# Attention products half a slot later, and output rows that alternate between two accumulators

## The chip, the core and the metric

The kernel runs on one core of one Trainium2 chip. The metric is device time in microseconds (us). Engines are named as in the profile: PE is TensorE (PEld its weight loads), DVE is VectorE, ACT is ScalarE, POOL is GpSimd, SP issues the DMAs. "L354" is line 354 of the kernel before.

## What is computed

A transformer block: attention with 32 query heads over cached keys and values, then a gated MLP, both behind a modulated layer norm.

```python
x = A_x                                         # (1, 2048, 576)
mod = (silu(c) @ w_mod).reshape(1, 6, 1, -1)    # shifts sa, sb, scales ca, cb, gates ga, gb
h = layernorm(x) * (1 + ca) + sa
q = (h @ wq) per head                           # 32 heads of 128
k, v = the last 512 rows of the caches          # 16 heads, each for two query heads
o = softmax(q k^T / sqrt(128)) v
x = x + ga * (o @ wo)
h = layernorm(x) * (1 + cb) + sb
x = x + gb * ((silu(h @ w1) * (h @ w3)) @ w2)   # 576 -> 4608 -> 576
```

All matrices are float32. The kernel splits each operand into a high and a low half of float16 and adds three products (high by high, high by low, low by high).

## The kernel before

The order of the instructions on every engine is the order in which the code issues them; each engine works its own list strictly in turn and waits where an operand or a buffer isn't ready.

Attention goes through 128 **slots**. A slot `i` is one query head on one block of 512 rows (`slots[i] = (u, j, b)`: group `u` of one key head, `j` which of its two query heads, `b` the block). Slots come in pairs, `j = 0` and `j = 1` on the same block. A slot has four **quarters** `t` (128 rows each). The main loop issues, per quarter:

- `scores(i, t)` (L401): three matmuls of `qT` with the keys into a PSUM bank; then DVE takes the maximum of each row (L405) and scales it (L406).
- `normalize(i - 2)` in the second quarter, DVE: for `j = 0` the low half of the values' product (L486), whose high half `take_first` makes on ACT (L479, first quarter); for `j = 1` the product times the inverse sums (L489), which `split_on` splits in the fourth quarter (L505, L506).
- `query_low(i + 1)` in the fourth quarter (L391, DVE): the low half of the next slot's `qT`.
- `weights(i, t)` (L418, ACT): the exponent, from the PSUM bank of the scores into `p`. `half_high` (L443, ACT) and `half_low` (L448, POOL) split `p` into `hp`, of which there are four buffers.
- `query(i + 1, t)` in the first three quarters (L343, L347): 14 matmuls of the next slot's projection into one bank (`pq`); with the last of them the high half of `qT` on ACT (L385).
- `attend_out` (L354, `back`): six matmuls that multiply one 128-row piece of an earlier pair with the output weights, into the accumulator `E` (`pe`, two PSUM banks). A row of the pair takes two pieces, one for each head; after the second, DVE adds the row to `acc` (L514). Second pieces fall in the second and fourth quarter.
- tasks at `(i, t)`: everything else that a table puts at that place: loads, peaks and scalings of weights, the making of the MLP's weights. Sums over partitions (L247, L1051, L1084) are matmuls into columns of `E` that the output rows don't use.
- `turn_away` (L455, SP): the DMA transposes of `hp` into `ptw`, two quarters after the scores. `ptw` has two buffers, one for a slot.

At the end of slot `i` comes `values(i - 1)` (L468): twelve matmuls of the values with `ptw` into a bank `po`. The PSUM's eight banks: two for `pq` and `po` (tag A), two for the scores of odd quarters (tag S), two for those of even quarters (`t_bank`, `pt`), two for `E`. `t_bank` also serves the transposes of the layer norm's rows in some slots.

The MLP's first products join in slot 127 (`stream`); after attention it has the rest of the time, and its down products alternate between `E` and two banks that replace `t_bank`'s.

Of the kernel before, what the change touches and what calls it, by code (L numbers as in the profile page):

```python
# [9 lines left out]
F32 = mybir.dt.float32  # L10
# [4 lines left out]
ALU = mybir.AluOpType  # L15
AX = mybir.AxisListType
PSUM = bass.MemoryType.PSUM
DRAM = bass.MemoryType.DRAM

P = 128  # L20
# [3 lines left out]
S = 2048  # L24
SB = 512
NSB = S // SB
ST = SB // P
# [5 lines left out]
HALF = D // 2  # L33
# [14 lines left out]
def tile_block(  # L48
# [19 lines left out]
    psum = ctx.enter_context(tc.tile_pool(name="psum", bufs=2, space=PSUM))  # L68
# [6 lines left out]
    def bank(tag, name):  # L75
        return psum.tile([P, 512], F32, tag=tag, name=name)


    E = psum.tile([P, 2, 512], F32, tag="E", name="pe", bufs=1)
    turning = ExitStack()  # L80
    tpool = turning.enter_context(tc.tile_pool(name="tpool", bufs=2, space=PSUM))

    def t_bank():
        return tpool.tile([P, 512], F32, tag="T", name="pt")

    def half_split(a):
        return a.rearrange("p (a n) -> p a n", a=2)
# [258 lines left out]
            else:  # L346
                nc.tensor.matmul(ps, w[:, k, DC, :], hT[:, 2 * DC, :], start=False, stop=k == 1)  # L347

    def back(o, w, t, first, last):

        rows = slice(t * P, (t + 1) * P)
        for n, (x, y) in enumerate(((0, 0), (0, 1), (1, 0))):
            for h in range(2):
                nc.tensor.matmul(  # L354
                    E[:, h, :HALF],
                    o[:, x, rows],
                    w[:, y, h * HALF : (h + 1) * HALF],
                    start=first and n == 0,
                    stop=last and n == 2,
                )  # L360
# [9 lines left out]
    slots = [(u, j, b) for u, (_, blocks, _) in enumerate(uses) for b in blocks for j in range(2)]  # L370
    begins = [next(i for i, slot in enumerate(slots) if slot[0] == u) for u in range(len(uses))]
    n = len(slots)
    state = [dict() for _ in range(n)]
    hT, wqs, keys, vals, wos = {}, {}, {}, {}, {}
# [14 lines left out]
    def query_low(i):  # L389
        q, ps = state[i]["qT"], state[i].pop("q")  # L390
        nc.vector.scalar_tensor_tensor(q[:, 1], ps, Q_DOWN, q[:, 0], op0=ALU.mult, op1=ALU.subtract)  # L391

    def scores(i, t):
        u, j, b = slots[i]
        g = uses[u][0]
        st = state[i]
        k, q = keys[u], st["qT"]
        rows = slice(t * P, (t + 1) * P)
        pss = bank("S", "pss") if t % 2 else t_bank()
        for n, (x, y) in enumerate(((0, 0), (0, 1), (1, 0))):  # L400
            nc.tensor.matmul(pss, q[:, x, rows], k[:, y, :], start=n == 0, stop=n == 2)  # L401
        m = (i * ST + t) % 3
        nm = nms[:, 2 * m : 2 * m + 2]
        factor = factors[:, g, j : j + 1]
        nc.vector.tensor_reduce(nm[:, 0:1], pss, axis=AX.X, op=ALU.max, negate=True)  # L405
        nc.vector.tensor_scalar(nm[:, 1:2], nm[:, 0:1], factor, P_LOG, op0=ALU.mult, op1=ALU.add)  # L406
        st["max", t] = pss, nm

    def weights(i, t):

        u, j, b = slots[i]
        factor = factors[:, uses[u][0], j : j + 1]
        st = state[i]
        pss, nm = st.pop(("max", t))
        if t == 0:
            st["l"] = odd.tile([P, 6 * ST], F32, tag="l", name="l", bufs=4) if j == 0 else state[i - 1]["l"]
        p = pool.tile([P, SB], F32, tag="p", name="p", bufs=PB)
        nc.scalar.activation(p, pss, AF.Exp, bias=nm[:, 1:2], scale=factor, accum_out=st["l"][:, j * ST + t : j * ST + t + 1])  # L418
        st["p", t] = p
# [20 lines left out]
    def half_high(i, t):  # L440

        hp = state[i]["hp", t] = pool.tile([P, 2, SB], F16, tag="hf", name="hp", bufs=HF)
        nc.scalar.copy(hp[:, 0, :], state[i]["p", t])  # L443

    def half_low(i, t):

        hp = state[i]["hp", t]
        nc.gpsimd.tensor_sub(hp[:, 1, :], state[i].pop(("p", t)), hp[:, 0, :])  # L448

    def turn_away(i, t):  # L450

        if t == 0:
            state[i]["pt"] = pool.tile([P, 2, KC, SB], F16, tag="pt", name="ptw")
        pt = state[i]["pt"]
        nc.sync.dma_start_transpose(  # L455
            out=pt.rearrange("p x c n -> p (x c) n")[:, :, t * P : (t + 1) * P],
            in_=state[i].pop(("hp", t)).rearrange("p x k -> p (x k)"),
        )

    def values(i):  # L460
        u, j, b = slots[i]
        st = state[i]
        v = vals[u]
        pt = st["pt"]
        po = bank("A", "po")
        for c in range(KC):
            for n, (x, y) in enumerate(((0, 0), (1, 0), (0, 1))):
                nc.tensor.matmul(  # L468
                    po, v[:, x, c, :], pt[:, y, c, :], start=c == 0 and n == 0, stop=c == KC - 1 and n == 2
                )  # L470
        st["po"] = po

    def new_o(i):
        return pool.tile([P, 2, SB], F16, tag=("ah", "al")[i % 2], name="o", bufs=3)

    def take_first(i):
        st = state[i]
        o = st["o"] = new_o(i)
        nc.scalar.activation(o[:, 0, :], st["po"], AF.Copy, scale=O_DOWN)  # L479

    def normalize(i):
        st = state[i]
        po = st.pop("po")
        if slots[i][1] == 0:
            o = st["o"]
            nc.vector.scalar_tensor_tensor(o[:, 1, :], po, O_DOWN, o[:, 0, :], op0=ALU.mult, op1=ALU.subtract)  # L486
            return
        on = st["on"] = pool.tile([P, SB], F32, tag="raw", name="on", bufs=RB)
        nc.vector.tensor_mul(  # L489
            on.rearrange("d (t p) -> d t p", t=ST),  # L490
            po.rearrange("d (t p) -> d t p", t=ST),
            st["r"].rearrange("d p t -> d t p"),
        )

    def split_on(i):
# [9 lines left out]
        nc.scalar.copy(o[:, 0, :], on)  # L505
        nc.gpsimd.tensor_sub(o[:, 1, :], on, o[:, 0, :])  # L506

    def attend_out(pair, t, j, total):
        u, _, b = slots[2 * pair]
        back(state[2 * pair + j]["o"], wos[u][:, j], t, j == 0, j == 1)  # L510
        if j == 1:
            run(*total)
            a = half_split(acc[b][:, t, :])
            nc.vector.scalar_tensor_tensor(  # L514
                a, E[:, :, :HALF], state[2 * pair]["l"][:, 5 * ST + t : 5 * ST + t + 1], a, op0=ALU.mult, op1=ALU.add
            )


# [457 lines left out]
    def run(i, t):  # L976
        for task, args in tasks.pop((i, t), ()):
            task(*args)
# [54 lines left out]
    lane = [0, ()]  # L1033
# [141 lines left out]
    for u, (g, blocks, whole) in enumerate(uses):  # L1175
# [8 lines left out]
        if u:  # L1184
            A = dict(load=-22, keys=-17, wq=-13, total=-9, scale=-9, put=-8, turn=-5, vals=-1)
            if u == 1:
                A.update(load=-16, keys=-13, wq=-13)
            A = {k: R + v for k, v in A.items()}
# [66 lines left out]
    for late in range(turns):  # L1255
        number = ITEMS + 4 * late
        loader, maker, w, _ = items[number]
        total = 2 * len(ORDER) * (late + 1) + ORDER.index("p3")
# [99 lines left out]
    for c in range(3):  # L1358
        i = 117 + 3 * c
# [112 lines left out]
    for i in range(n + 2):  # L1472
        run(i, -1)
        for t in range(ST):
            if t > 1 and i < n:
                turn_away(i, t - 2)
            if t < 2 and 1 <= i <= n:
                turn_away(i - 1, t + 2)
            if i < n:
                scores(i, t)  # L1480
            if 2 <= i <= n and t == 1:
                normalize(i - 2)
            if t == 3 and i + 1 < n:
                query_low(i + 1)
            if i < n:
                weights(i, t)
            if i < n:
                half_high(i, t)
                half_low(i, t)
            if 2 <= i <= n + 1 and t == 0 and slots[i - 2][1] == 0:  # L1490
                take_first(i - 2)
            if 1 <= i <= n and t < 2:
                sums(i - 1, t)
            if 2 <= i <= n and t == 3:
                split_on(i - 2)
            if i + 1 < n and t < ST - 1:
                query(i + 1, t)
            if i >= m0:
                for _ in range(3 if (i, t) == (n + 1, 0) else 1):
                    next(stream)  # L1500
            for piece in outs.get((i, t), ()):
                attend_out(*piece, (i, ("total", t)))
            run(i, ("total", t))
            run(i, ("taken", t))
            run(i, t)
            if 1 <= i <= n and t == 2:
                sums(i - 1, t)
            run(i, t)
        if 1 <= i <= n:
            values(i - 1)  # L1510
        if i == n:
            normalize(n - 1)
            split_on(n - 1)
    turning.close()
    after = ctx.enter_context(tc.tile_pool(name="after", bufs=1, space=PSUM))
    lane[1] = (E, after.tile([P, 2, 512], F32, tag="T2", name="pf"))
    for _ in stream:
        pass
    for i in (1, 0):
# [58 lines left out]
```

## Time and profile before

| | us |
|---|---|
| median of 3 runs | 2823.19 (2821.3 to 2827.48) |
| the profiled execution | 2823.43 |
| its span | 2821.6 |
| PE busy | 2678.1 (95%) |
| DVE busy | 1971.4 (70%) |
| ACT busy | 1637.1 (58%) |
| POOL busy | 1935.5 (69%) |

The span runs from the first to the last instruction. A busy time is the sum over an engine's instructions, without those that only wait or issue a DMA. In a row of a group, the count and the mean of one instruction stand behind the shapes, then the busy time, then the engine's idle time just ahead of these instructions with what ended it. A matmul's row shows 0.38 us for 512 columns, but the next one starts 0.22 us after it: they overlap, so the time that a row of matmuls takes is best read from start to start.

### The profile page before, as it was taken

The numbers are of one execution on the slowest core, as the hardware profiler recorded it, in microseconds if no ns is written. First come the engines' busy times: TensorE is split into PE (matmuls) and PEld (weight loads), VectorE is DVE, ScalarE is ACT, GpSimd is POOL, SyncE is SP. The second block draws the span as 40 slices with busy tenths as digits, with TensorE's granted clock in tenths as the row PEclk, the third lists the DMA queues.
The fourth block names the chain that finished last, engine by engine and source line by source line (L and its number), as shares of the span: only waits on it lengthen the run. The fifth ranks groups of instructions, "written<-read, shape, count | busy, mean of one in ns | idle before, by whom it ended". The sixth has DMA issues, their size and how long they took to land. (4 is left out here: it accounts for less than half of the span.)

```text
span 2821.6 us, 44006 instructions
## 1 busy us (share of the span) xinstructions
PE 2678.1 (95%) x15024; PEld 1480.2 (52%) x15024; DVE 1971.4 (70%) x3492; ACT 1637.1 (58%) x3022; POOL 1935.5 (69%) x1793
## 2 busy tenths in 40 slices
PE   6899999999999999999999899999999999999998
PEld 3455555555455554545554455555555555555555
DVE  6776777777778777777775548777776565656666
ACT  4687777778687877868676634544443333333332
POOL 4577788989799887877768726688874355334435
PEclk9999999999999999999999999999999999999999
DMA  5778888878798898989989954555644443333332
GB/s 168 178 169 186 202 197 183 194 173 207 157 195 196 191 207 179 226 175 225 212 195 215 200 162 159 191 185 190 213 136 125 148 127 122 109 104 109 104 111 76
DMA packets 711153, 479.86 MB, mean 170 GB/s; under 512 B 568080, under 2 KB 597904, under 8 KB 710160
## 3 DMA queue, kind: packets, MB, share of 16 engines
q1 hardware_dynamic: 710320, 477.05, 67.4%
q8 instruction: 118, 1.93, 0.3%
q14 instruction: 107, 0.88, 0.1%
q10 hardware_dynamic: 608, 0.00, 0.0%
HBM read 246.83 MB, written 95.86 MB: 121 GB/s over the span
## 5 line engine op out<-in xcount | busy, mean ns | idle before, releaser
L448 POOL TENSOR_TENSOR hp<-p,hp 128x512 f16<-128x512 f32 x512 | 595.0, 1166 | 292.0 <-ACT hp L443 159.0
L771 PEld LDWEIGHTS <-wset 128*128 128x128 f16 x3528 | 344.9, 98 | 336.8 <-issue 2.7
L354 PE MATMUL pe<-o 128*128 128x288 f16 x3072 | 464.2, 288 | 30.4 <-DVE acc L514 23.6
L771 PE MATMUL py<-hset,wset 128*128 128x512 f16 x2016 | 482.7, 380 | 1.8 <-ACT u L951 1.8
L468 PE MATMUL po<-ptw,v 128*128 128x512 f16 x1536 | 369.1, 392 | 61.0 <-DMA ptw<-hp 45.7
L354 PEld LDWEIGHTS <-o 128*128 128x128 f16 x3072 | 301.4, 98 | 210.1 <-issue 42.3
L418 ACT ACTIVATE p<-pt,table,factors 128x512 f32<-128x512 f32 x256 | 198.3, 775 | 324.0 <-DVE table L406 286.4
L771 PE MATMUL px<-hset,wset 128*128 128x512 f16 x1512 | 361.6, 379 | 0.0
L443 ACT CAST hp<-p 128x512 f16<-128x512 f32 x512 | 316.4, 618 | 35.7 <-DMA ptw<-hp 18.8
L92 POOL TENSOR_TENSOR akv<-u,akv 128x512 f16<-128x512 f32 x141 | 164.8, 1177 | 175.0 <-ACT akv L91 167.1
L405 DVE TENSOR_REDUCE table<-pss 128x1 f32<-128x512 f32 x256 | 176.1, 688 | 154.6 <-PE pss L401 154.4
L343 PE MATMUL pq<-hT,wq 128*128 128x512 f16 x1092 | 281.4, 380 | 0.0
L468 PEld LDWEIGHTS <-v 128*128 128x128 f16 x1536 | 151.7, 102 | 237.2 <-issue 63.7
L405 DVE TENSOR_REDUCE table<-pt 128x1 f32<-128x512 f32 x256 | 174.4, 681 | 90.5 <-PE pt L401 90.1
L418 ACT ACTIVATE p<-pss,table,factors 128x512 f32<-128x512 f32 x256 | 197.9, 773 | 35.9 <-DVE table L406 33.3
L856 PEld LDWEIGHTS <-akv 128*128 128x128 f16 x1728 | 169.2, 98 | 93.8 <-issue 4.5
L514 DVE SCALAR_TENSOR_TENSOR acc<-pe,l,acc 128x576 f32<-128x576 f32 x256 | 207.5, 811 | 15.5 <-PE pe L354 12.9
L401 PE MATMUL pt<-k,qT 128*128 128x512 f16 x768 | 210.9, 382 | 6.9 <-ACT qT L385 3.2
L401 PEld LDWEIGHTS <-qT 128*128 128x128 f16 x1536 | 151.0, 100 | 126.5 <-DVE qT L391 8.1
L401 PE MATMUL pss<-k,qT 128*128 128x512 f16 x768 | 212.2, 386 | 0.0
L343 PEld LDWEIGHTS <-wq 128*128 128x128 f16 x1104 | 108.4, 98 | 139.5 <-issue 9.8
L850 DVE SCALAR_TENSOR_TENSOR acc<-pf,table,acc 128x576 f32<-128x576 f32 x140 | 113.5, 811 | 80.6 <-PE pf L856 80.6
(232 smaller groups left out, 4738.5 us busy)
## 6 DMA issues: line engine op xcount, KB each, us to landing
wset<-wd SPq DMA_DIRECT2D x213, 320.0 KB, 3.2
oset<-od SPq DMA_DIRECT2D x106, 288.0 KB, 3.2
wraw<-in_w SPq DMA_DIRECT2D x36, 768.0 KB, 5.3
wd<-wmade SPq DMA_DIRECT2D x75, 320.0 KB, 3.3
r<-row SPq DMA_DIRECT2D x64, 256.0 KB, 4.0
wset<-wd SPq DMA_DIRECT2D x71, 160.0 KB, 2.2
w2raw<-in_w SPq DMA_DIRECT2D x19, 576.0 KB, 5.4
wd<-ring SPq DMA_DIRECT2D x33, 320.0 KB, 2.8
```

Source lines behind the costliest of these rows:

```text
L92: eng.tensor_sub(halves[:, 1], src, halves[:, 0])
L343: nc.tensor.matmul(ps, w[:, k // 2, m, :], hT[:, DC + m if k == 1 else m, :], start=s == 0, stop=False)
L354: nc.tensor.matmul(E[:, h, :HALF], o[:, x, rows], w[:, y, h * HALF : (h + 1) * HALF], start=first and n == 0, stop=last and n == 2,)
L401: nc.tensor.matmul(pss, q[:, x, rows], k[:, y, :], start=n == 0, stop=n == 2)
L405: nc.vector.tensor_reduce(nm[:, 0:1], pss, axis=AX.X, op=ALU.max, negate=True)
L418: nc.scalar.activation(p, pss, AF.Exp, bias=nm[:, 1:2], scale=factor, accum_out=st["l"][:, j * ST + t : j * ST + t + 1])
L443: nc.scalar.copy(hp[:, 0, :], state[i]["p", t])
L448: nc.gpsimd.tensor_sub(hp[:, 1, :], state[i].pop(("p", t)), hp[:, 0, :])
L468: nc.tensor.matmul(po, v[:, x, c, :], pt[:, y, c, :], start=c == 0 and n == 0, stop=c == KC - 1 and n == 2)
L514: nc.vector.scalar_tensor_tensor(a, E[:, :, :HALF], state[2 * pair]["l"][:, 5 * ST + t : 5 * ST + t + 1], a, op0=ALU.mult, op1=ALU.add)
L771: nc.tensor.matmul(ps, w[:, a, :], h[:, b, :], start=start and n == 0, stop=stop and n == 6, skip_group_check=True)
L856: nc.tensor.matmul(ps[:, h, :HALF], a[:, rows], w[:, b, :], start=m == 0, stop=m == 2)
```

## The change

Three things. The values' products move from the end of the slot to the second quarter of the next one (`values(i - 2)` at `t == 1`, ahead of that quarter's output products); the normalization and the high half that go with them move to the third quarter. The output products of odd rows go into a second accumulator `E2`, outside of the slots in `TURNS`. `E2` takes the two banks that scores of even quarters had; scores of all quarters now alternate between the two banks of tag S, and `t_bank` hands out halves of `E2` in the slots in `TURNS`, and for the last two slots' values.

```diff
     E = psum.tile([P, 2, 512], F32, tag="E", name="pe", bufs=1)
-    turning = ExitStack()
-    tpool = turning.enter_context(tc.tile_pool(name="tpool", bufs=2, space=PSUM))
+    E2 = psum.tile([P, 2, 512], F32, tag="E2", name="pt", bufs=1)
+    t_banks = [0]
     def t_bank():
-        return tpool.tile([P, 512], F32, tag="T", name="pt")
+        t_banks[0] += 1
+        return E2[:, t_banks[0] % 2, :]
...
-    def back(o, w, t, first, last):
+    def back(ps, o, w, t, first, last):
...
-                    E[:, h, :HALF],
+                    ps[:, h, :HALF],
...
-        pss = bank("S", "pss") if t % 2 else t_bank()
+        pss = bank("S", "pss")
...
-        po = bank("A", "po")
+        po = bank("A", "po") if i < len(slots) - 2 else t_bank()
...
+    TURNS = (*range(15), *range(104, 121), n, n + 1)
     def attend_out(pair, t, j, total):
         u, _, b = slots[2 * pair]
-        back(state[2 * pair + j]["o"], wos[u][:, j], t, j == 0, j == 1)
+        ps = E2 if t % 2 and total[0] not in TURNS else E
+        back(ps, state[2 * pair + j]["o"], wos[u][:, j], t, j == 0, j == 1)
...
-                a, E[:, :, :HALF], ...
+                a, ps[:, :, :HALF], ...
...
-            if 2 <= i <= n and t == 1:
+            if 2 <= i <= n and t == 2:
+                if slots[i - 2][1] == 0:
+                    take_first(i - 2)
                 normalize(i - 2)
...
-            if 2 <= i <= n + 1 and t == 0 and slots[i - 2][1] == 0:
-                take_first(i - 2)
...
+            if 2 <= i <= n and t == 1:
+                values(i - 2)
             for piece in outs.get((i, t), ()):
                 attend_out(*piece, (i, ("total", t)))
...
-        if 1 <= i <= n:
-            values(i - 1)
         if i == n:
+            values(n - 1)
...
-    lane[1] = (E, after.tile([P, 2, 512], F32, tag="T2", name="pf"))
+    lane[1] = (E, E2)
```

On TensorE, at the end of slot 102 (`o` are output products' operands, `v` the values, `qT` the scores' operand), before:

```order
L354 LDWEIGHTS o
L354 MATMUL pe<-o 128x288
L468 LDWEIGHTS v
L468 MATMUL po<-ptw,v 128x512
...
L401 LDWEIGHTS qT
L401 MATMUL pt<-k,qT 128x512
```

and of the change:

```order
L402 LDWEIGHTS qT
L402 MATMUL pss<-k,qT 128x512
L355 LDWEIGHTS o
L355 MATMUL pe<-o 128x288
...
L402 LDWEIGHTS qT
L402 MATMUL pss<-k,qT 128x512
```

The values' twelve matmuls no longer stand between the output products of the fourth quarter and the next slot's scores; they stand ahead of the output products of the second quarter.

On VectorE, from the second quarter's maximum in slot 102 to the next slot's first, before:

```order
L405 TENSOR_REDUCE table<-pss 128x1
L406 TENSOR_SCALAR table<-table,factors 128x1
L486 SCALAR_TENSOR_TENSOR o<-po,o 128x512
L514 SCALAR_TENSOR_TENSOR acc_87<-pe,l,acc_87 128x576
L405 TENSOR_REDUCE table<-pt 128x1
L406 TENSOR_SCALAR table<-table,factors 128x1
L405 TENSOR_REDUCE table<-pss 128x1
L406 TENSOR_SCALAR table<-table,factors 128x1
L391 SCALAR_TENSOR_TENSOR qT<-pq,qT 128x512
L514 SCALAR_TENSOR_TENSOR acc_88<-pe,l,acc_88 128x576
L405 TENSOR_REDUCE table<-pt 128x1
```

and of the change:

```order
L406 TENSOR_REDUCE table<-pss 128x1
L407 TENSOR_SCALAR table<-table,factors 128x1
L518 SCALAR_TENSOR_TENSOR acc_85<-pt,l,acc_85 128x576
L406 TENSOR_REDUCE table<-pss 128x1
L407 TENSOR_SCALAR table<-table,factors 128x1
L487 SCALAR_TENSOR_TENSOR o<-po,o 128x512
L406 TENSOR_REDUCE table<-pss 128x1
L407 TENSOR_SCALAR table<-table,factors 128x1
L392 SCALAR_TENSOR_TENSOR qT<-pq,qT 128x512
L518 SCALAR_TENSOR_TENSOR acc_86<-pe,l,acc_86 128x576
L406 TENSOR_REDUCE table<-pss 128x1
```

The normalization's low half (L486, now L487) moved from ahead of the second quarter's `acc` to behind the third quarter's maximum. In slot 102 no task stands between the second quarter's `acc` and the third quarter's maximum; in other slots the tasks at the second quarter stand there, before and after. On ScalarE the values' high half (L479, now L480) moved from behind the first quarter's cast to just ahead of the third quarter's exponent; the exponent, the cast and the high half of `qT` follow each other as before. The orders of POOL and SP are the same.

More of the change, by code (lines that the diff above doesn't have):

```diff
@@ L514, in attend_out @@
             nc.vector.scalar_tensor_tensor(
-                a, E[:, :, :HALF], state[2 * pair]["l"][:, 5 * ST + t : 5 * ST + t + 1], a, op0=ALU.mult, op1=ALU.add
+                a, ps[:, :, :HALF], state[2 * pair]["l"][:, 5 * ST + t : 5 * ST + t + 1], a, op0=ALU.mult, op1=ALU.add
             )
@@ L1508, in tile_block @@
             run(i, t)
-        if 1 <= i <= n:
-            values(i - 1)
         if i == n:
+            values(n - 1)
             normalize(n - 1)
             split_on(n - 1)
-    turning.close()
-    after = ctx.enter_context(tc.tile_pool(name="after", bufs=1, space=PSUM))
-    lane[1] = (E, after.tile([P, 2, 512], F32, tag="T2", name="pf"))
+    lane[1] = (E, E2)
     for _ in stream:
```

## The prediction

> **What bounds the kernel now.** I read the head of the page first, then the waits of TensorE, the groups by line, the busy time by stage, and last the order of time within one undisturbed slot. A slot is one head on one block of 512 rows; there are 128, each of four quarters.
>
> ```profile
> span 2821.6 us, 44006 instructions
> ...
> PE 2678.1 (95%) x15024; PEld 1480.2 (52%) x15024; DVE 1971.4 (70%) x3492; ACT 1637.1 (58%) x3022; POOL 1935.5 (69%) x1793
> ```
>
> TensorE (PE) is busy for 95% of the span, so only its pauses can be won, and a new pause on it is paid in full. The pauses that the change aims at:
>
> ```profile
> PE po L468 <- DMA ptw<-hp: 45.7, 27, 5.5
> PE pe L354 <- DVE acc L514: 23.6, 22, 2.7
> ```
>
> The columns are total us, times, longest us. Products with the values (`po`, L468) wait for the transposed weights `ptw`; output products (`pe`, L354) wait until VectorE has emptied their one accumulator into `acc`.
>
> ```profile
> L354 PE MATMUL pe<-o 128*128 128x288 f16 x3072 | 464.2, 288 | 30.4 <-DVE acc L514 23.6 <-DVE table L1087 4.7 <-DVE table L1057 1.2
> L468 PE MATMUL po<-ptw,v 128*128 128x512 f16 x1536 | 369.1, 392 | 61.0 <-DMA ptw<-hp 45.7 <-issue 6.9 <-DMA row<-l 5.1
> L401 PE MATMUL pss<-k,qT 128*128 128x512 f16 x768 | 212.2, 386 | 0.0
> L401 PE MATMUL pt<-k,qT 128*128 128x512 f16 x768 | 210.9, 382 | 6.9 <-ACT qT L385 3.2 <-DVE hf L207 2.0 <-ACT hf L209 0.6
> L514 DVE SCALAR_TENSOR_TENSOR acc<-pe,l,acc 128x576 f32<-128x576 f32 x256 | 207.5, 811 | 15.5 <-PE pe L354 12.9 <-PE pe L1051 2.2
> L405 DVE TENSOR_REDUCE table<-pss 128x1 f32<-128x512 f32 x256 | 176.1, 688 | 154.6 <-PE pss L401 154.4
> L406 DVE TENSOR_SCALAR table<-table,factors 128x1 f32<-128x1 f32 x512 | 109.6, 214 | 27.0
> L391 DVE SCALAR_TENSOR_TENSOR qT<-pq,qT 128x512 f16<-128x512 f32 x127 | 87.7, 690 | 102.1 <-ACT qT L385 101.9
> ```
>
> After the second bar stands the idle time before the group: 61.0 us before values, 30.4 us before output products, next to nothing before scores (L401). The stage of attention, in stretches (PE, PEld, DVE, ACT, POOL busy, clock, DMA):
>
> ```profile
> 39.00:254.00 215.00, 188.02 (x969) 99.03 (x970) 157.44 (x329) 153.87 (x288) 134.18 (x124) 0.94 0.73 168
> 254.00:1037.00 783.00, 743.42 (x4100) 401.46 (x4098) 592.69 (x1181) 604.92 (x1158) 685.87 (x660) 0.98 0.84 188
> 1037.00:1331.00 294.00, 276.95 (x1529) 148.83 (x1528) 219.40 (x443) 220.09 (x425) 230.83 (x208) 0.99 0.90 202
> 1331.00:1625.00 294.00, 272.73 (x1533) 149.41 (x1532) 197.62 (x404) 201.02 (x393) 219.55 (x208) 0.98 0.95 209
> ```
>
> 127 slots start between 39 and 1625 us: 12.5 us each. An undisturbed one, slot 102, in order of time:
>
> ```profile
> 1308.43 0.81 PE L401 MATMUL pt<-k,qT 128*128 128x512 f16 x3
> ...
> 1312.60 1.32 SPq L455 DMA_TRANSPOSE ptw<-hp  x1
> ...
> 1313.36 0.81 PE L401 MATMUL pt<-k,qT 128*128 128x512 f16 x3
> ...
> 1313.56 0.82 DVE L514 SCALAR_TENSOR_TENSOR acc<-pe,l,acc 128x576 f32<-128x576 f32 x1 [0.28 <-PE pe L354]
> ...
> 1314.01 0.60 PE L343 MATMUL pq<-hT,wq 128*128 128x512 f16 x2
> ...
> 1314.30 0.68 DVE L405 TENSOR_REDUCE table<-pt 128x1 f32<-128x512 f32 x1
> ...
> 1314.87 0.90 PE L354 MATMUL pe<-o 128*128 128x288 f16 x6
> ...
> 1315.32 0.78 ACT L418 ACTIVATE p<-pt,table,factors 128x512 f32<-128x512 f32 x1 [0.29 <-DVE table L406]
> ...
> 1315.61 0.81 PE L401 MATMUL pss<-k,qT 128*128 128x512 f16 x3
> ...
> 1316.22 0.62 ACT L443 CAST hp<-p 128x512 f16<-128x512 f32 x1
> 1316.25 0.90 PE L354 MATMUL pe<-o 128*128 128x288 f16 x6
> ...
> 1316.75 0.59 ACT L385 ACTIVATE qT<-pq 128x512 f16<-128x512 f32 x1
> ...
> 1316.99 2.75 PE L468 MATMUL po<-ptw,v 128*128 128x512 f16 x12
> ...
> 1317.37 0.69 DVE L391 SCALAR_TENSOR_TENSOR qT<-pq,qT 128x512 f16<-128x512 f32 x1
> ...
> 1319.58 0.81 PE L401 MATMUL pt<-k,qT 128*128 128x512 f16 x3
> ```
>
> From start to start the slot takes 1319.58 - 1308.43 = 11.15 us: TensorE's floor. So 127 x (12.5 - 11.15) = 171 us is all that attention could give.
>
> The rows also show a chain that costs nothing today. The next slot's scores (1319.58) read `qT`. It is made by: scores of the third quarter (1313.36), maximum on VectorE (L405), exponent (L418) and cast (L443) on ScalarE, then in ScalarE's order the high half of `qT` (L385), then on VectorE its low half (L391, done at 1318.06). That is 4.70 us. TensorE takes 6.22 us over the same way, of which 2.59 us (1316.99 to 1319.58) are the values' products.
>
> **The change, part by part.**
>
> *Values half a slot later.* They start some 4.2 us later in TensorE's work: behind a first quarter, (11.15 - 6.22) / 2 = 2.46 us, and behind scores and query of a second, the same less its output products, 2.46 - 0.74 (1314.87 to 1315.61) = 1.72 us. Waits of up to 5.5 us shrink to little. Removed: 61.0 us idle plus the stretch of the groups themselves, 369.1 - 128 x 2.75 (the undisturbed row) = 17, together 78 us. 10 us of it stay, for the few waits over 4.2 us.
>
> *Rows in two accumulators.* Removed: 30.4 + 464.2 - 512 x 0.90 = 34 us; 5 us stay, in the slots listed in `TURNS` and where a sum is taken in the accumulator of the next row. VectorE's own 0.81 us a row is unchanged and off TensorE's path. By the Trainium skill, "Perfetto Trace Analysis", section "Optimizing Tensor Performance", matmul groups should rotate through banks so that emptying one overlaps the next; the 23.6 us wait agrees, and the same rule speaks against taking two banks from the scores.
>
> *What the values covered.* Without them TensorE is at the next slot's scores 6.22 - 2.59 = 3.63 us after the third quarter's, and at their third matmul, which needs the low half, 0.43 us later (0.81 less one matmul of 0.38): 4.06 us. The chain needs 4.70 us and a hand-over of 0.03 (1317.34 to 1317.37), so even slot 102 pauses 0.67 us. The order of ScalarE and VectorE leaves no way around it: `qT` stands behind this exponent and cast on the one, behind the fourth quarter's maximum on the other.
>
> Two things lengthen the chain. VectorE's second-quarter tasks stand behind that quarter's `acc`, which waits for output products that now end just as the third quarter's scores begin. They can't run under the values, since VectorE works in order. Its load from 254 to 1037 us is 592.69 / 64 = 9.3 us a slot; four maxima with their scalings (4 x 0.90), L391 (0.69), two L514 (1.62) and the normalization (0.7, as L391, to 1.1) make 6.8, so 2.5 us a slot are tasks: 0.6 a quarter. Second, ScalarE is at times late; it gets the values' 2.6 us to catch up, so I keep 0.15 us. Sum: 0.67 + 0.6 + 0.15 = 1.42 us, in 126 slots 179 us. From below the price is 0.67 (no task in the way). From above it is what the chain takes on average today, from the start of the third quarter's scores to the end of L391: 6.2 us over 127 slots, first and last:
>
> ```profile
> 42.83 0.81 PE L401 MATMUL pt<-k,qT 128*128 128x512 f16 x3
> ...
> 47.92 0.69 DVE L391 SCALAR_TENSOR_TENSOR qT<-pq,qT 128x512 f16<-128x512 f32 x1 [0.91 <-ACT qT L385]
> ...
> 1612.26 0.81 PE L401 MATMUL pt<-k,qT 128*128 128x512 f16 x3
> ...
> 1616.27 0.69 DVE L391 SCALAR_TENSOR_TENSOR qT<-pq,qT 128x512 f16<-128x512 f32 x1
> ```
>
> That gives 6.2 - 4.06 = 2.1 us a slot, 270 us. I take 1.42, nearer the lower end, since the queues get the pause itself to run empty. The chain pauses TensorE already in some slots, with the cover:
>
> ```profile
> PEld L401 <- DVE qT L391: 8.1, 18, 0.6
> ```
>
> Those 8 us, and the 6.9 us of idle time before the scores in `pt`, lie at the same place, are contained in the new pause and come off it.
>
> *Scores in two banks.* Scores now need the exponent of two quarters before. For the next slot's first quarter that is the third quarter's, done 1315.32 + 0.78 - 1313.36 = 2.74 us after, against 3.63: covered, and earlier in the same chain than `qT`. If that cover goes, `qT` is later still, so it adds nothing of its own.
>
> *Normalization and its high half one or two quarters later.* Same instructions. The 0.69 us on VectorE leaves the way of the second quarter's `acc`, and falls while ScalarE works on the exponent; the high half (ScalarE) goes ahead of that exponent, while it would wait for the maximum. Nothing, unless ScalarE is late: then 0.6 us in every other slot, within the range.
>
> *The transposes' queue.* `ptw` has two tiles, so SP's first transpose of a slot now waits until the values of two slots before are done, about 6.9 us into the slot, not 4.2 (1312.60 in slot 102). What stands behind it on SP (loads, stores) moves by up to 2.7 us. The four `hp` tiles hide it: the tile is wanted again a slot later. If not, ScalarE's cast waits and with it the chain.
>
> *The clock.* After one long pause the same matmuls were slower:
>
> ```profile
> 725.85 1.32 PE L354 MATMUL pe<-o 128*128 128x288 f16 x6 [2.36 <-DVE table L1087]
> ...
> 728.25 1.56 PE L354 MATMUL pe<-o 128*128 128x288 f16 x6
> ```
>
> 1.32 and 1.56 us instead of 0.90: at least 1.1 us, after 2.36 us of idling. Pauses of 1.4 us should not do that; for one slot in ten, with a long VectorE task in the way, I add 1.3 us: 13 us. The Trainium skill, "TensorE: Matmul & The Clock Gate", section "Why this matters for your kernels", puts the limit at idle gaps of about 3 us; the trace shows it at 2.4. By the page's limit most of the 13 us would fall away.
>
> Sum: 179 + 13 = 192 us new; 78 - 10 + 34 - 5 + 8 + 7 = 112 us gone; + 80 us. The profiled execution took 2823.4 us (span 2821.6), the median of the runs is 2823.2. Forecast: 2903 us.
>
> **The rivals.**
>
> *A: the cover was not needed.* If VectorE's tasks mostly run earlier and ScalarE is never late, the pause is the 0.67 us of slot 102: 84 us against 112 gone, 2795 us. For it: slot 102 is an ordinary slot but for the tasks. Against: the 18 waits that exist with 2.59 us of cover, and tasks that can't overtake. It decides at 112 / 126 = 0.89 us a slot: below that the kernel is faster.
>
> *B: the chain stays as long as today.* 270 us, the clock twice as often (26 us), less 112: + 184 us, 3007 us. For it: busy VectorE, ScalarE and POOL (685.87 of 783 us) that a shorter slot would press further. Against: each pause relieves them.
>
> *C: the transposes were not what values waited for, but POOL.* POOL at 88% makes the low halves; if its lag only grows, the waits return in the second quarter: up to 40 of the 78 us, 2943 us. But slots that are longer, not shorter, let POOL catch up. It lies within the forecast's range.
>
> **How the numbers follow.** Forecast with C: 0.74, between a pause of 1.0 us (2837) and one of 1.9 us with twice the clock's part (2976). A: 0.11. B: 0.15. The range 2835 to 2985 leaves out A and most of B; where the sign is the same in 0.89 of the cases, it is the forecast's own range but for 9 us. Faster by over 0.2%, about what a measurement of this kernel can tell from no change: 0.08 (A); within 0.2%: 0.03; slower: 0.89.
>
> **What would show it.** In the profile after: idle before L402 (scores), or before its weight loads, released by `qT` from ScalarE and VectorE, of some 100 us or more and in nearly every slot; idle before values under 15 us and before output products under 10 us; the second half, after 1700 us, unchanged at 1121 us; attention at about 13.1 us a slot. I am wrong if scores hardly wait for `qT`, or if they wait chiefly for the exponent of two quarters before (the banks).

## The result and the profile after

| | before | after |
|---|---|---|
| median, us | 2822.24 (2817.5 to 2827.48, 4 runs) | 2907.26 (2905.45 to 2909.11, 4 runs) |
| after / before | | 1.0301 [1.0280, 1.0321] |
| the profiled execution, us | 2823.43 | 2905.51 |
| its span | 2821.6 | 2903.6 |

The change costs 85 us; the forecast was 2903. One of the ten executions of E1 below took 3477.56 us at a granted clock of 0.753; no median and no ratio here counts it. The head of the page after, which answers to the two lines of before:

```profile
span 2903.6 us, 43942 instructions
...
PE 2700.1 (93%) x15024; PEld 1470.7 (51%) x15024; DVE 1951.3 (67%) x3492; ACT 1642.2 (57%) x3022; POOL 1936.1 (67%) x1793
```

The work is the same; TensorE's share of it fell from 95% to 93%. Where the pauses are now, by line (busy time, mean ns, then the idle time ahead of the group and what ended it):

```profile
L402 PE MATMUL pss<-k,qT 128*128 128x512 f16 x1536 | 444.6, 385 | 151.8 <-ACT qT L386 114.2 <-DVE qT L392 21.9 <-ACT p L419 4.4
L469 PE MATMUL po<-ptw,v 128*128 128x512 f16 x1512 | 346.9, 379 | 0.0
L355 PE MATMUL pe<-o 128*128 128x288 f16 x1920 | 288.6, 287 | 5.1 <-DVE acc L518 4.7 <-DVE us L234 0.4
L355 PE MATMUL pt<-o 128*128 128x288 f16 x1152 | 175.1, 289 | 0.0
```

The 61.0 us ahead of the values and most of the 30.4 us ahead of the output products are gone; scores, which waited for next to nothing, have 151.8 us ahead of them, nearly all released by `qT`. TensorE's waits and those of its weight loads say how often (total us, times, longest us; a pause can stand in both lists):

```profile
PE pss L402 <- ACT qT L386: 114.2, 120, 4.9
PE pss L402 <- DVE qT L392: 21.9, 31, 2.1
PE pss L402 <- ACT p L419: 4.4, 5, 1.1
```

```profile
PEld L402 <- ACT qT L386: 144.5, 121, 5.2
PEld L402 <- DVE qT L392: 96.5, 127, 2.6
```

The low half (L392) holds the weight load of the third scores' matmul in all 127 slots. The boundary between slots 102 and 103, in order of time:

```profile
1380.16 0.81 PE L402 MATMUL pss<-k,qT 128*128 128x512 f16 x3
...
1381.10 0.68 DVE L406 TENSOR_REDUCE table<-pss 128x1 f32<-128x512 f32 x1
...
1382.12 0.78 ACT L419 ACTIVATE p<-pss,table,factors 128x512 f32<-128x512 f32 x1 [1.90 <-DVE table L407]
...
1383.02 0.62 ACT L444 CAST hp<-p 128x512 f16<-128x512 f32 x1
1383.06 0.90 PE L355 MATMUL pe<-o 128*128 128x288 f16 x6
...
1383.55 0.59 ACT L386 ACTIVATE qT<-pq 128x512 f16<-128x512 f32 x1
...
1384.17 0.69 DVE L392 SCALAR_TENSOR_TENSOR qT<-pq,qT 128x512 f16<-128x512 f32 x1
1384.19 1.12 PE L402 MATMUL pss<-k,qT 128*128 128x512 f16 x3 [0.24 <-ACT qT L386]
...
1384.92 0.10 PEld L402 LDWEIGHTS <-qT 128*128 128x128 f16 x1 [0.61 <-DVE qT L392]
```

This is the chain of the forecast, link by link, from the third quarter's scores (1380.16) to the low half (1384.86). The output products end, the high half lands, the scores start; then their third matmul waits again, for the low half: the three take 1.12 us instead of 0.81. The slot, from 1372.34 to 1384.19, takes 11.85 us; the same slot took 11.15 before. A calm slot loses 0.70 us.

The next table is worked out from the traces: the time that attention's 127 slots lose, from the start of each matmul to the next, over 0.216 us for 512 columns and 0.122 for 288 (the spacing inside an undisturbed group), put down to the group that started late.

| attention, us | a slot | lost before scores | values | output products |
|---|---|---|---|---|
| before 1585.9 | 12.49 | 18 | 85 | 36 |
| after 1662.8 | 13.09 | 200 | 0 | 7 |

Of the 200 us, 189 lie at the slots' first scores: 134 at the first matmul and 54 at the third. After attention nothing changed (busy times of PE, PEld, DVE, ACT, POOL; clock, DMA share and GB/s at the end), before and then after:

```profile
1700.00:2821.60 1121.60, 1107.71 (x6417) 628.14 (x6415) 736.94 (x1002) 415.10 (x697) 630.30 (x555) 1.00 0.43 138
```

```profile
1782.00:2903.60 1121.60, 1107.44 (x6424) 629.24 (x6422) 738.06 (x1004) 415.85 (x698) 631.39 (x555) 1.00 0.44 138
```

### The profile page after: what moved, and what is told of

Read it like the earlier page. It is cut to its first block, busy times and chain, and to the rows that moved or that the text cites. A ratio compares the mean times of both kernels' runs of the same rounds, so it can differ in the third digit from the quotient of the medians.

```text
span 2903.6 us, 43942 instructions
## 1 busy us (share of the span) xinstructions
PE 2700.1 (93%) x15024; PEld 1470.7 (51%) x15024; DVE 1951.3 (67%) x3492; ACT 1642.2 (57%) x3022; POOL 1936.1 (67%) x1793
## 5 line engine op out<-in xcount | busy, mean ns | idle before, releaser
L419 ACT ACTIVATE p<-pss,table,factors 128x512 f32<-128x512 f32 x512 | 396.5, 774 | 397.9 <-DVE table L407 375.5
L402 PE MATMUL pss<-k,qT 128*128 128x512 f16 x1536 | 444.6, 385 | 151.8 <-ACT qT L386 114.2
L406 DVE TENSOR_REDUCE table<-pss 128x1 f32<-128x512 f32 x512 | 349.2, 682 | 77.1 <-PE pss L402 74.9
L469 PE MATMUL po<-ptw,v 128*128 128x512 f16 x1512 | 346.9, 379 | 0.0
L402 PEld LDWEIGHTS <-qT 128*128 128x128 f16 x1536 | 141.5, 100 | 312.8 <-ACT qT L386 144.5
L355 PE MATMUL pe<-o 128*128 128x288 f16 x1920 | 288.6, 287 | 5.1 <-DVE acc L518 4.7
L518 DVE SCALAR_TENSOR_TENSOR acc<-pt,l,acc 128x576 f32<-128x576 f32 x96 | 78.5, 818 | 267.6 <-PE pt L355 267.6
L518 DVE SCALAR_TENSOR_TENSOR acc<-pe,l,acc 128x576 f32<-128x576 f32 x160 | 129.7, 810 | 91.9 <-PE pe L355 73.0
L355 PE MATMUL pt<-o 128*128 128x288 f16 x1152 | 175.1, 289 | 0.0
L854 DVE SCALAR_TENSOR_TENSOR acc<-pt,table,acc 128x576 f32<-128x576 f32 x140 | 113.5, 811 | 80.2 <-PE pt L860 80.2
L955 ACT COPY u<-py 128x512 f32<-128x512 f32 x72 | 42.2, 586 | 200.4 <-PE py L775 198.5
```

Source lines behind the costliest of these rows:

```text
L355: nc.tensor.matmul(ps[:, h, :HALF], o[:, x, rows], w[:, y, h * HALF : (h + 1) * HALF], start=first and n == 0, stop=last and n == 2,)
L469: nc.tensor.matmul(po, v[:, x, c, :], pt[:, y, c, :], start=c == 0 and n == 0, stop=c == KC - 1 and n == 2)
L518: nc.vector.scalar_tensor_tensor(a, ps[:, :, :HALF], state[2 * pair]["l"][:, 5 * ST + t : 5 * ST + t + 1], a, op0=ALU.mult, op1=ALU.add)
```

## The experiments

Each diff is against the changed kernel, but for the two marked "on the kernel before". The ratio is to the kernel before, beside which each was timed (its median was 2821.4 to 2823.6). The losses are those of the table above, worked out in the same way from the one profiled execution of each; that of E11 (2860.01 us) was the fastest of its four, so its losses look some 10 us small.

| | median us | ratio | scores | values | output |
|---|---|---|---|---|---|
| E1 values back at the end | 2820.23 | 0.9994 [0.9981, 1.0006] | 42 | 82 | 7 |
| E2 the move alone | 2921.11 | 1.0351 [1.0329, 1.0373] | 207 | 0 | 12 |
| E3 `qT` earlier | 2821.44 | 1.0000 [0.9990, 1.0009] | 107 | 1 | 21 |
| E4 high half twice | 2982.59 | 1.0568 [1.0547, 1.0589] | 258 | 0 | 14 |
| E5 high half twice, before | 2853.27 | 1.0094 [1.0077, 1.0111] | 37 | 69 | 55 |
| E3b `qT` earlier, before | 2807.45 | 0.9938 [0.9923, 0.9953] | 9 | 86 | 25 |
| E7 the move and `qT` earlier | 2847.88 | 1.0084 [1.0067, 1.0100] | 37 | 0 | 116 |
| E11 tasks ahead | 2869.79 | 1.0165 [1.0145, 1.0184] | 152 | 2 | 4 |
| E12 tasks ahead, `qT` earlier | 2809.61 | 0.9958 [0.9945, 0.9971] | 87 | 2 | 18 |
| E10 values at the end, `qT` earlier | 2804.74 | 0.9941 [0.9928, 0.9954] | 25 | 80 | 7 |
| E6 the order spread evenly | 2793.41 | 0.9889 [0.9874, 0.9905] | 83 | 3 | 11 |

### Which part costs: E1 and E2

E1 puts the values, the normalization and its high half back to where they were, and keeps the accumulators and the banks.

```diff
-            if 2 <= i <= n and t == 1:
-                values(i - 2)
...
+        if 1 <= i <= n:
+            values(i - 1)
```

> Only the banks change: the values' products are back at the end of the slot (and the normalization in the second quarter), the two output accumulators and the two score banks stay. Theory 'cover' (the time was lost because the values no longer lie between the third quarter's scores and the next slot's): the wait of scores for qT falls from some 240 us of late weight loads to under 20 us, the waits of values for their transposes come back (60 to 85 us), output products wait under 10 us; 2785 to 2815 us, a little below before. Rival 'banks' (scores in two banks instead of four hold TensorE up): 2880 us or more, with scores waiting for the exponent (ACT p).

E2 keeps the move and takes back `E2`: one accumulator, scores in four banks.

```diff
-        pss = bank("S", "pss")
+        pss = bank("S", "pss") if t % 2 else t_bank()
...
-        ps = E2 if t % 2 and total[0] not in TURNS else E
-        back(ps, state[2 * pair + j]["o"], wos[u][:, j], t, j == 0, j == 1)
+        back(state[2 * pair + j]["o"], wos[u][:, j], t, j == 0, j == 1)
```

> Only the move: values in the second quarter of the next slot, normalization in the third; one output accumulator and four score banks as before. 'Cover': 2905 to 2940 us, scores wait for qT as in the changed kernel (PE idle before them 130 us or more), values do not wait, output products wait 5 to 35 us. 'Banks': 2790 to 2830 us, scores hardly wait.

E2 is slower than the change by 14 us, E1 takes the kernel before's time: the loss is the move's, as the theory of the cover said. The waits of E2:

```profile
PE pt L401 <- ACT qT L385: 123.4, 120, 4.8
PE pt L401 <- DVE qT L391: 21.2, 31, 2.1
...
PE pe L354 <- DVE acc L514: 4.6, 5, 1.6
```

The last line was not foreseen. With the move alone, output products already wait for no more than 4.6 us (23.6 before): the pause ahead of the scores gives VectorE time to empty the one accumulator. That this pause is the reason fits E7 below, which has the move with little of the pause left, and where the accumulator holds TensorE for 60.6 us. And E1 missed its time, 5 us above the range, since two accumulators alone bring nothing:

```profile
PE pss L402 <- ACT p L419: 24.0, 23, 2.6
...
PE pe L355 <- DVE acc L518: 6.7, 7, 1.6
```

Output products wait for `acc` 17 us less, and scores now wait 24 us for the exponent that must free one of their two banks. The banks moved the wait; they removed little of it.

### Is it a chain that was covered: E3, E4, E5, E3b

If `qT` is made a quarter earlier, the chain of exponent, cast and `qT` no longer ends at the slot's end. E3 issues the last part of the projection ahead of the third quarter's exponent and the low half behind it, with the same instructions.

```diff
+            if i + 1 < n and t == ST - 2:
+                query(i + 1, t)
+                query_low(i + 1)
...
-            if t == 3 and i + 1 < n:
-                query_low(i + 1)
...
-            if i + 1 < n and t < ST - 1:
+            if i + 1 < n and t < ST - 2:
                 query(i + 1, t)
```

> The changed kernel with the last part of the query, and with it qT's high half on ScalarE, issued ahead of the third quarter's exponent, and its low half on VectorE straight after that quarter's maximum. TensorE's order stays. 'Cover': the chain to qT shrinks from 4.7 to about 3.1 us at best, under the 4.06 us that TensorE needs, so most of the 190 us pause goes; the exponent of two quarters before is next (2.74 us plus VectorE's tasks against 3.63): 2740 to 2800 us, below both kernels. 'Banks': within 30 us of the changed kernel, 2880 us or more, because that exponent gets later by the 0.5 us of qT.

86 us come back, against the 85 that the change cost, but the time stops 21 us above the range. TensorE's waits in E3, and those of its weight loads:

```profile
PE pss L402 <- ACT p L419: 79.4, 89, 4.2
PE pe L355 <- DVE acc L518: 17.4, 17, 2.1
```

```profile
PEld L402 <- ACT qT L386: 16.4, 21, 3.3
```

The wait for `qT` is all but gone (144.5 to 16.4 us); the exponent stands next in line, through the two banks. The prediction had it covered, 2.74 us against 3.63, and had not priced how close it comes: with the high half of `qT` now ahead of it on ScalarE, and in every other slot the values' high half too, it ends 3.46 us after the third quarter's scores in slot 102 and 2.98 in slot 103, calm slots both.

E4 makes the chain longer by one instruction of ScalarE, the high half written a second time. E5 does the same on the kernel before.

```diff
             nc.scalar.activation(q[:, 0], ps, AF.Copy, scale=Q_DOWN)
+            nc.scalar.activation(q[:, 0], ps, AF.Copy, scale=Q_DOWN)
```

> The changed kernel with the high half of qT written twice by ScalarE (the same values), 0.53 us more in the chain in each of 127 slots. 'Cover': the whole of it shows, +55 to +75 us over the changed kernel, 2960 to 2985 us. 'Banks': the exponents are not on this way, so it is mostly hidden: under +25 us.

> The kernel before with the high half of qT written twice, 0.53 us more in the chain, as in the changed kernel, where it cost 75 us. 'Cover': before, the values' products hide most of it (1.3 us of slack at the median, 18 slots with none): +5 to +25 us, 2827 to 2847 us. Rival (ScalarE itself is short of time, wherever the instruction stands): +60 us or more.

In the changed kernel the instruction costs 75.3 us, or 0.59 us in each of 127 slots: its whole duration (0.59 us in the rows of slot 102). In the kernel before it costs 30 us, 6 us above the range that was expected: scores and output products lose some 19 us more each, values some 16 less. The cover takes up more than half. The waits there:

```profile
PE pe L354 <- DVE acc L515: 35.2, 35, 2.7
PE po L469 <- DMA ptw<-hp: 34.6, 23, 4.3
PE pt L402 <- ACT qT L386: 14.5, 19, 2.8
```

A chain that pays the whole of an added instruction bounds the kernel in nearly every slot; one that pays less than half bounds it in some slots only. E3b is E3's edit on the kernel before.

> The kernel before with the early qT. 'Cover': qT is hidden there already, all but some 10 us; 2805 to 2825 us. If the early qT were a gain of its own (ScalarE and VectorE idle less), it would show here too: under 2790 us.

It gains 16 us, where the same edit gained 86 in the changed kernel. There scores had lost little (18 us, now 9); output products lose 11 us less.

### Which link is late: E11 and E12

The prediction put 0.6 us a slot on VectorE's second-quarter tasks, which stand ahead of the third quarter's maximum. E11 issues them ahead of the values and the output products, in slots 15 to 103.

```diff
+            ahead = t == 1 and i not in TURNS and i < n
+            if ahead:
+                run(i, ("total", t))
+                run(i, ("taken", t))
+                run(i, t)
             if 2 <= i <= n and t == 1:
                 values(i - 2)
```

> The changed kernel with the tasks of the second quarter issued ahead of that quarter's values and output products (in the 89 slots 15 to 103, where the sums' accumulator is free), so that VectorE does them while TensorE works on the values and not behind the output row. Only VectorE's and TensorE's orders change. It tests one term of the sum, VectorE's tasks in the chain, put at 0.6 us a slot: those tasks take 59 us in these slots in the trace of before, so 30 to 60 us faster than the changed kernel, 2847 to 2877 us. If the chain is long for another reason (ScalarE late, and the tasks' time hidden behind that), under 15 us faster.

37 us less than the changed kernel, within its range. In slots 16 to 79, where the tasks are densest, a slot falls from 12.88 us to 12.39, by 0.5 us. The waits for the high half:

```profile
PE pss L402 <- ACT qT L386: 71.8, 105, 3.4
```

114.2 us became 71.8. At the slots' first scores 145 us are still lost, 1.15 us a slot: the 0.70 of a calm slot, and lateness that these tasks don't explain. E12 does it on top of E3.

> Early qT and the tasks ahead together, on the changed kernel. With the early qT alone, scores still lost some 107 us, mostly to the exponent of two quarters before, which VectorE's tasks delay. If the tasks are the cause, 25 to 50 us faster than with the early qT alone, 2770 to 2797 us, with the wait for exponents at 30 to 60 us instead of 79. If the two banks are short whatever VectorE does, within 15 us of 2821.

It gains 12 us over E3 and stops 13 us above its range; its rival, within 15 us of E3, is what came. The exponent still holds the banks:

```profile
PE pss L402 <- ACT p L419: 64.7, 76, 4.3
```

VectorE's second-quarter tasks are the smaller part of it. The third quarter's maximum starts 1.17 us after its scores (1.52 in E3; 0.93 in calm slots), so 0.24 us of lateness are left there. The exponent ends 3.80 us after the scores, 0.82 later than in calm slots of odd number such as 103: 0.58 of that arises behind the maximum, on ScalarE. Slot 102 of E12 shows how, with TensorE and ScalarE in order of time:

```profile
1294.64 0.81 PE L402 MATMUL pss<-k,qT 128*128 128x512 f16 x3
...
1296.35 0.60 ACT L386 ACTIVATE qT<-pq 128x512 f16<-128x512 f32 x1 [0.90 <-PE pq L348]
...
1296.84 0.59 ACT L480 ACTIVATE o<-po 128x512 f16<-128x512 f32 x1
...
1297.32 0.78 ACT L419 ACTIVATE p<-pss,table,factors 128x512 f32<-128x512 f32 x1
```

The scaled maximum is done at 1296.50, but two instructions stand ahead of the exponent: the high half of `qT`, which E3's edit put there, and the values' high half (L480), which the change put there in every other slot. The exponent ends 3.46 us after the scores; the bank is wanted after 3.63. Over the 127 third quarters, 112 us lie between the scaled maximum and the exponent: 71 in the 58 slots where the values' high half stands right ahead of it, 40 in the 55 where that of `qT` does. No run changed this order by itself, so what it is worth in time stays open.

### What the second accumulator is worth: E7 and E10

E7 is the move with the early `qT`, one accumulator and four banks: E2's and E3's edits together.

```diff
-        pss = bank("S", "pss")
+        pss = bank("S", "pss") if t % 2 else t_bank()
...
-            if i + 1 < n and t < ST - 1:
+            if i + 1 < n and t < ST - 2:
```

> Only the move and the early qT (last query part and both halves of qT ahead of the third quarter's exponent); one output accumulator, four score banks as before. Theory 'next in line is the bank': what the early qT left in the changed kernel's banks (some 90 us of scores waiting for the exponent of two quarters before) is gone with four banks; scores lose under 25 us, values under 5 us, output products 20 to 50 us as they share one accumulator: 2745 to 2785 us. Rival 'a busy VectorE and ScalarE, whatever the banks': the pause turns up elsewhere on TensorE, 2805 to 2830 us.

A clear miss, 63 us above the range and 18 above its rival's. The banks are no longer short (37 us lost before scores), but with neither pause nor cover the one accumulator is:

```profile
PE pe L354 <- DVE acc L514: 60.6, 50, 3.0
PE pe L354 <- DVE us L233: 25.2, 15, 2.6
```

In the second row VectorE reads sums over partitions, which share `E`. Between E3 and E7 the second accumulator is worth 26 us, though it takes two banks from the scores. E10 has the values at the end (E1's edit), the second accumulator, two banks and the early `qT`.

```diff
-            if 2 <= i <= n and t == 1:
-                values(i - 2)
...
+        if 1 <= i <= n:
+            values(i - 1)
...
-            if i + 1 < n and t < ST - 1:
+            if i + 1 < n and t < ST - 2:
```

> Values at the end of the slot as before, two output accumulators, two score banks, and the early qT. It tells whether the move is worth anything once qT is early: values should again lose some 80 us. Theory 'the move pays only with the cover replaced': 2795 to 2815 us, above the evenly laid-out variant's 2793. Rival 'the move never pays': 2785 us or less.

It lies within its range, and is 17 us faster than E3, which differs from it by the move alone. Even with `qT` early the move costs more before the scores (107 us lost against 25) than it saves before the values (1 against 80).

### A place for everything: E6

E6 keeps the move and the accumulators, and spreads the rest: the projection as 7 and 7 matmuls in the first and second quarter, `qT`'s high half with the second and its low half in the third, the values in the third quarter and their normalization in the fourth; SP's first transpose is issued behind the values.

```diff
-    QP = (range(0, 5), range(5, 10), range(10, 14))
+    QP = (range(0, 7), range(7, 14))
...
-            if t == 3 and i + 1 < n:
+            if t == 2 and i + 1 < n:
                 query_low(i + 1)
...
-            if 2 <= i <= n and t == 1:
+            if 2 <= i <= n and t == 2:
                 values(i - 2)
+            if t == 2 and i < n:
+                turn_away(i, 0)
```

> The changed kernel's banks, with the work laid out so that two banks are enough: the query in two parts of seven matmuls in the first and second quarters, qT's high half in the second and its low half in the third, the values in the third quarter, their normalization in the fourth. From scores to the scores that reuse their bank TensorE now has 4.3 to 6.9 us everywhere, against 2.74 us and VectorE's tasks. 'Next in line is the bank': scores lose under 30 us, values under 10 us, output products under 15 us: 2725 to 2775 us, the fastest. Rival 'busy engines': 2800 us or more, with waits for the exponent or for SP's transposes, which now wait for the values of the third quarter.

It is the fastest of all, 1.1% under the kernel before, and still 18 us above its range (and 7 below its rival's). Its waits on TensorE, ScalarE and SP's queue:

```profile
PE pss L402 <- ACT p L419: 66.5, 68, 5.6
```

```profile
ACT hp L444 <- DMA ptw<-hp: 78.6, 66, 2.8
```

```profile
SPq L456 <- PE po L469: 200.0, 80, 6.5
```

Read upwards: the transposes wait until the values have left one of the two `ptw` tiles, the cast waits for a transpose to free its `hp` tile, and the exponents behind that cast come late for the banks. This is a part of it only. Followed back from each of the 68 waits of the first row along ScalarE's work to its last idle time of over 0.15 us, some 13 of the 66.5 us begin at an instruction that waited for a transpose, and some 43 at an exponent that waited for VectorE's scaled maximum. No run tells these causes apart.

## Why the prediction was right

**The pause.** Forecast 1.42 us in 126 slots, 179 us; the trace shows 189 us at that place, 1.50 a slot. Its three parts:

- The calm slot: 0.67 forecast, 0.70 in slot 102.
- VectorE's second-quarter tasks: 0.6 forecast. The third quarter's maximum starts 1.51 us after its scores on average, 0.58 later than in calm slots, and E11 took 0.5 us a slot away by moving the tasks.
- ScalarE: 0.15 forecast. The chain takes 5.65 us on average, 0.95 over the calm 4.70; 0.58 of it is VectorE's above, so 0.37 is left. Some 0.17 of that lies between the scaled maximum and the exponent: in 16 slots, with 19 us, the values' high half stands right ahead of the exponent there, the case that the prediction put at nothing unless ScalarE is late. The rest lies behind the exponent, with a link that the prediction left out: third-quarter tasks on VectorE, which stand ahead of the fourth quarter's maximum and so of the low half. VectorE in slot 65, where that cost most of a pause of 2.08 us:

```profile
906.57 1.08 DVE L490 TENSOR_TENSOR on<-po,r 128x512 f32<-128x512 f32 x1
...
907.56 1.50 DVE L1153 TENSOR_TENSOR oraw<-oraw,gate_a 128x576 f32<-128x576 f32 x1
...
908.98 0.94 DVE L1046 TENSOR_REDUCE table<-wraw 128x1 f32<-128x768 f32 x1
...
909.84 0.68 DVE L406 TENSOR_REDUCE table<-pss 128x1 f32<-128x512 f32 x1
...
910.76 0.68 DVE L392 SCALAR_TENSOR_TENSOR qT<-pq,qT 128x512 f16<-128x512 f32 x1
```

The fourth quarter's scores start at 906.05, their maximum 3.8 us later.

The three measured parts add up to 1.65 us. The pause is shorter, 1.50, since TensorE's own way there takes 3.8 us on average without the pause, not the 3.63 of slot 102. The step that put 0.15 us was under-sized; the total is within 10 us.

**The cover.** "What the values covered" is the step on which the sign rested. E2 (the move alone loses), E4 and E5 (75 against 30 us for one added instruction) and E3 (the loss goes when `qT` is early) show it.

**Values.** 78 us less 10 were to go; 85 went and nothing stayed. By the idle times alone (61.0 to 0.0) the forecast was near; no wait was left.

**Two accumulators.** 34 us less 5 forecast, 29 measured: the right number for the wrong reason. E2 shows that the move alone removes most of it, E1 that the accumulators alone are worth nothing in time, and only with the pause out of the way (E3 against E7) are they worth 26 us. The step added two effects that share one wait.

**Two banks.** "Adds nothing of its own" held in the changed kernel (4.4 us) and only there: 24.0 us in E1, 79.4 in E3. The pause for `qT` hid it.

**The transposes' queue.** Hidden by the four `hp` tiles, as forecast: SP's queue waits for the values now, which it did not before, and ScalarE's cast loses little by it (18.8 us before, 32.0 after):

```profile
SPq L456 <- PE po L469: 124.5, 72, 5.0
```

```profile
ACT hp L443 <- DMA ptw<-hp: 18.8, 20, 3.7
```

```profile
ACT hp L444 <- DMA ptw<-hp: 32.0, 25, 3.7
```

**The clock.** 13 us forecast, though one of 126 slots in ten at 1.3 us would be 16. Among 1397 starts within the query's matmuls, 44 come over 0.25 us after the last, against 6 before, and they lose 13.2 us against 5.1: 8 us, without those in scores and output products. One such place is shown below.

**The rivals.** A (the cover not needed) needed a pause under 0.89 us; E11 comes nearest, with VectorE's tasks out of the way, and with 1.15 us it is still 48 us slower than before. B (the chain as long as today, 6.2 us) did not come: it took 5.65. The prediction's reason, that the pauses let the queues run empty, was not tested by itself. C (values wait again) did not come: 0.0 us.

The sum of the changes measured start to start, +182 before scores, -85, -29 and +10 in the query, is +78 us; attention as a whole grew by 76.8, the profiled span by 82. The other 5 us lie behind the start of slot 127. That the total came so near the forecast's +80 is in part luck. The forecast had 179 us of pause less 15 that lay there already, 164 net, and of those 15 the trace of before shows some 10 at the slots' first scores; against 182 it was 18 short. It was also 17 short for the values, 68 against 85, and the two errors cancel.

## What to carry to other kernels

A group of matmuls that waits may itself be the cover of a chain that no row shows as a wait. Before moving it, add up the chain that runs beside it, from the last matmul that starts it to the next that needs it, and compare it with what TensorE has left to do there: 3.63 us of work against 4.70 us of chain showed a pause here, of 0.67 us, from one undisturbed slot. That did not yet tell the sign, which turned at 0.89 us: the lateness of the busy slots decided it, 1.50 us on average. Shortening the chain paid with the values where they were (16 us in E3b, 17 in E10); with the move, only the layout of E6 came out below that, 11 us under E10. And count PSUM banks at the place where they are next in line: a bank given to one group can be a wait for another.

## What the runs showed of the hardware

TensorE's clock fell after pauses that were each shorter than the 2.36 us of the prediction. At the end of the same slot 65, the scores of slot 66 wait twice:

```profile
908.81 0.61 PE L402 MATMUL pss<-k,qT 128*128 128x512 f16 x2 [1.22 <-ACT qT L386]
911.50 0.61 PE L402 MATMUL pss<-k,qT 128*128 128x512 f16 x1 [2.08 <-DVE qT L392]
911.90 2.34 PE L344 MATMUL pq<-hT,wq 128*128 128x512 f16 x5
```

Five matmuls that take 1.24 us elsewhere take 2.34. The granted clock in stretches there (the number after the five busy times):

```profile
904.00:908.00 4.00, 3.59 (x22) 1.95 (x20) 3.89 (x7) 1.23 (x3) 3.84 (x4) 1.00 0.34 66
908.00:911.90 3.90, 1.01 (x4) 0.25 (x5) 3.79 (x7) 2.47 (x6) 3.82 (x4) 0.80 0.61 152
911.90:914.30 2.40, 2.40 (x8) 0.93 (x7) 2.33 (x8) 1.01 (x2) 1.81 (x3) 0.50 1.05 215
```

1.00 before the pauses, 0.50 behind them. Elsewhere a pause of 1.98 us was enough, with one of 0.28 us behind it, ahead of the scores' third matmul:

```profile
431.83 1.34 PE L402 MATMUL pss<-k,qT 128*128 128x512 f16 x3 [1.98 <-ACT qT L386]
432.96 2.34 PE L344 MATMUL pq<-hT,wq 128*128 128x512 f16 x5
```

The granted clock from 433.0 to 435.4 us was 0.50 there too. In a kernel whose every slot pauses, these are few: behind 15 of attention's 52 idle times of over a microsecond on TensorE the next matmuls were slow, while behind two of 2.25 us they were not. What tells the two apart is open.
